# Ln and Exp in place of Newton roots, and a longer hand-written start, in an attention and MLP kernel

## The chip, the cores and the metric

The kernel runs on one core of a Trainium2 chip. The metric is the device time of one execution in microseconds (us), as the median of several executions; the kernel before takes 655.64 us (654.83 to 656.18). The spans quoted from profiles are about 1.8 us shorter than the device times of the same executions.

The engines go by their short names: PE is TensorE, DVE is VectorE, ACT is ScalarE, POOL is GpSimd, SP is SyncE, which here only issues DMAs.

## The reference

There are 8 batches, 12 heads, 448 tokens and a head size of 64. The model width is 768, the hidden width of the MLP 3072.

```python
def rmsnorm(x, g):
    return x / np.sqrt(np.mean(x * x, axis=-1, keepdims=True) + 1e-06) * g
q_n, k_n = rmsnorm(q, g_q), rmsnorm(k, g_k)
attn = softmax(q_n @ k_n.transpose(0, 1, 3, 2) / 8)      # shortened
x = (attn @ v).transpose(0, 2, 1, 3).reshape(8, 448, 768)

mu  = np.mean(x, axis=-1, keepdims=True)
var = np.mean((x - mu) ** 2, axis=-1, keepdims=True)
xn  = (x - mu) / np.sqrt(var + 1e-06) * g_ln
out = x + np.maximum(xn @ w_ch1, 0.0) @ w_ch2
```

Each row needs an inverse square root three times: for q, for k and for the LayerNorm.

## The kernel before

The work is cut into *pairs* of heads (six to a batch, numbered through: pair 6 is the first of batch 1) and *units* of one or two pairs that are loaded and prepared together. Units 0 to 3 are batch 0, units 4 to 6 are batch 1. Preparing a unit means: squares of q and k on ACT, row sums on DVE, the inverse roots, k times the product of the two gains, k split in a high and a low fp16 half, q scaled and copied twice, and the copy of v. Then q and k must be transposed. Units 0 to 4 are transposed by TensorE; from unit 5 on the DMA engines do it.

The program has two phases. In the first, a hand-written list gives the order of all pieces of batch 0's attention. A letter is a piece (b begin, a and c squares, d and e sums, f g h the root, i k times g, j k l m halves and scaled q, v the copy of v, K and Q transposes, S scores, V values, T statistics, L loads, W weights) and a number its unit or pair. Then come 22 matmuls without use, which are meant to keep TensorE's clock up through the first LayerNorm. In the second phase each batch's MLP runs with the next batch's attention spread beside it by a formula.

```python
POOL_HI, POOL_DUP, ACT_Q = (1, 2, 3), (3,), (0,)
ORDER = """
b0 c0 e0 fq0 gq0 a0 hq0 i0 d0 fk0 gk0 j0 b1 c1 a1 i1 l0 m0 k0 hk0 d1 K0 e1 j1 Q0 f1 S0.0 g1 k1
... (cut)
V5.3 V5.4 V5.5 V5.6 T5
""".split()
DMA_UNIT = 5

def _guess(nc, out, a):            # exp of the scaled bit pattern: a first guess of a ** -0.5
    nc.scalar.activation(out, a.bitcast(INT32), AFT.Exp, scale=-0.5 * LN2 * 2.0 ** -23,
                         bias=0.5 * LN2 * (127.0 - 0.043))

def _newton(nc, out, a, t, last=None):
    eng = nc.vector
    for i in range(2):
        eng.tensor_tensor(out=t, in0=out, in1=out, op=ALU.mult)
        eng.scalar_tensor_tensor(out=t, in0=t, scalar=-0.5, in1=a, op0=ALU.mult, op1=ALU.mult)
        eng.scalar_tensor_tensor(out=last if i and last is not None else out, in0=t, scalar=1.5,
                                 in1=out, op0=ALU.add, op1=ALU.mult)
... (cut)
        def kg():
            nc.gpsimd.tensor_tensor(out=c["t"][1], in0=c["t"][1],
                                    in1=sh.gprod.unsqueeze(1).broadcast_to([128, g, D]),
                                    op=ALU.mult)
... (cut)
        def dma_k():
            khl, kU = c["khl"].rearrange("p g e d -> p g (e d)"), self.kU[u % 2]
            ... (cut)
            nc.sync.dma_start_transpose(
                kU[:, 0:1536].rearrange("p (g c) -> p g c", c=128), khl[:, 0:12])
            for e in range(2):
                nc.sync.dma_start_transpose(...)     # the 64 left-over rows; cut
        def dma_q():
            q, qU = c["qn"].rearrange("p g e d -> p g (e d)"), self.qU[u % 2]
            for j in range(3):
                nc.sync.dma_start_transpose(
                    qU.rearrange("p w e s -> p (w e) s")[:, :, ts(j, 128)], q[:, 4 * j:4 * j + 4])
            for e in range(2):
                nc.sync.dma_start_transpose(qU[:, :, e, 384:S], q[64 * e:64 * e + 64, 12:14])
... (cut)
    def run_first(self):
        nc = self.nc
        self.steps, self.mark = self.attention()
        self.pos = 0
        self.first_attention()
        ps = self.ps_m.tile([128, 512], FP32, tag="mlp", name="psW")
        for _ in range(WARM):
            nc.tensor.matmul(ps[:, 0:384], self.sh.id16, ..., start=True, stop=True)
        for op in self.ln_ops(0):
            op()
```

So a unit from 5 on has eight DMA transposes, three for k and five for q, all issued by SyncE, and behind them in the same queue stand the loads of later units. The weights of the MLP are loaded by GpSimd, three pieces of the first matrix (W0 to W2) and two halves of the second (W3, W4). Pair 8 is the first of unit 5, and pair 10 the first of unit 6.

Of the kernel before, what the change touches and what calls it, by code (L numbers as in the profile page):

```python
# [28 lines left out]
POOL_HI, POOL_DUP, ACT_Q = (1, 2, 3), (3,), (0,)  # L29
# [5 lines left out]
b0 c0 e0 fq0 gq0 a0 hq0 i0 d0 fk0 gk0 j0 b1 c1 a1 i1 l0 m0 k0 hk0 d1 K0 e1 j1 Q0 f1 S0.0 g1 k1  # L35
h1 l1 m1 b2 a2 c2 i2 G L4 W0 S0.1 v0 S0.2 d2 K1 S0.3 j2 S0.4 W1 S0.5 W2 e2 f2 g2 Q1 h2 S0.6
V0.0 k2 l2 m2 S1.0 S1.1 b3 S1.2 a3 S1.3 V0.1 V0.2 v2 V0.3 S1.4 K2 V0.4 S1.5 Q2 c3 S1.6 V0.5
V0.6 S2.0 T0 S2.1 d3 V1.0 V1.1 S2.2 V1.2 S2.3 V1.3 e3 V1.4 i3 f3 g3 j3 V1.5 S2.4 h3 S2.5 K3 Q3
V1.6 k3 l3 m3 S2.6 v3 G2 L5 V2.0 S3.0 S3.1 K4 T1 V2.1 W3 S3.2 S3.3 W4 V2.2 V2.3 S3.4 V2.4 Q4
S3.5 V2.5 S3.6 V2.6 K5 S4.0 S4.1 Q5 V3.0 V3.1 S4.2 V3.2 S4.3 V3.3 S4.4 V3.4 S4.5 V3.5 S4.6  # L40
V3.6 S5.0 V4.0 V4.1 T3 S5.1 S5.2 V4.2 S5.3 V4.3 S5.4 V4.4 S5.5 V4.5 S5.6 V4.6 V5.0 V5.1 V5.2
V5.3 V5.4 V5.5 V5.6 T5
""".split()
DMA_UNIT = 5
LN2 = 0.6931471805599453
# [6 lines left out]
def _guess(nc, out, a):  # L52

    nc.scalar.activation(out, a.bitcast(INT32), AFT.Exp, scale=-0.5 * LN2 * 2.0 ** -23,  # L54
                         bias=0.5 * LN2 * (127.0 - 0.043))


def _newton(nc, out, a, t, last=None):

    eng = nc.vector  # L60
    for i in range(2):
        eng.tensor_tensor(out=t, in0=out, in1=out, op=ALU.mult)
        eng.scalar_tensor_tensor(out=t, in0=t, scalar=-0.5, in1=a, op0=ALU.mult, op1=ALU.mult)
        eng.scalar_tensor_tensor(out=last if i and last is not None else out, in0=t, scalar=1.5,
                                 in1=out, op0=ALU.add, op1=ALU.mult)


def _rsqrt(nc, out, a, t, eps, last=None, mul=1.0):

    nc.vector.tensor_scalar(out=a, in0=a, scalar1=mul, scalar2=eps, op0=ALU.mult, op1=ALU.add)  # L70
    _guess(nc, out, a)
    _newton(nc, out, a, t, last)
# [14 lines left out]
class _Fast:  # L87


    def __init__(self, ctx, tc, sh, q, k, v, g_ln, w1, w2, out):  # L90
# [35 lines left out]
        self.late = []  # L126
# [15 lines left out]
    def load_first(self):  # L142
        nc = self.nc
        flat = self.hT.rearrange("p f n -> p (f n)").bitcast(FP32)
        t = [flat[:, 2688 * n:2688 * n + 2688].rearrange("p (w g d) -> p w g d", w=NPAIR, d=D)
             for n in range(2)]
        v = self.p_in.tile([128, 3, 14, D], FP32, tag="qkv", name="vfirst")
        t.append(v.rearrange("p n g d -> p (n g d)").rearrange("p (w g d) -> p w g d", w=NPAIR,
                                                               d=D))
        main = lambda eng, n, p: self.load_main(eng, n, t[n][:, p, 0:6], 0, 2 * p, 2)  # L150
        left = lambda eng, n: self.load_left(eng, n, t[n][:, :, 6], 0, 0, H)
        for n in range(2):
            main(nc.sync, n, 0)
            left(nc.sync, n)
        for n, p in ((1, 1), (0, 1), (1, 2), (1, 3), (0, 2), (0, 3), (2, 0), (2, 1)):
            main(nc.sync, n, p)
        left(nc.sync, 2)
        for n, p in ((1, 4), (1, 5), (0, 4), (0, 5)):
            main(nc.sync, n, p)
        for p in range(2, NPAIR):  # L160
            main(nc.sync, 2, p)
        self.v_first = t[2]
        for u, (b, hs, m) in enumerate(UNITS):
            if b == 0:
                self.loads[u] = [x[:, hs // 2:hs // 2 + m].rearrange("p w g d -> p (w g) d")
                                 for x in t]
# [16 lines left out]
    def prep_ops(self, u):  # L183

# [8 lines left out]
        def begin():  # L193
            c["t"] = self.loads.pop(u)
            c["ssq"] = self.p_n.tile([128, 2, 14], FP32, tag="ssq", name="ssq")[:, :, 0:g]
            c["rr"] = self.p_n.tile([128, 2, 14], FP32, tag="rr", name="rr")[:, :, 0:g]
            c["rt"] = self.p_n.tile([128, 2, 14], FP32, tag="rt", name="rt")[:, :, 0:g]
            o = 7 * UNIT_PAIR[u]
            c["rf"] = self.rr[:, :, o:o + g]
            c["qn"] = self.p_n.tile([128, 14, 2, D], FP16, tag="qn", name="qn")[:, 0:g]  # L200
            c["khl"] = self.p_n.tile([128, 14, 2, D], FP16, tag="khl", name="khl")[:, 0:g]
            self.units[u] = (c["qn"], c["khl"], m)
# [10 lines left out]
        def eps(n=slice(0, 2)):  # L213
            nc.vector.tensor_scalar(out=c["ssq"][:, n], in0=c["ssq"][:, n], scalar1=D * 1e-6,
                                    scalar2=None, op0=ALU.add)

        def guess(n=slice(0, 2)):
            _guess(nc, c["rr"][:, n], c["ssq"][:, n])

        def root(n=slice(0, 2)):  # L220
            _newton(nc, c["rr"][:, n], c["ssq"][:, n], c["rt"][:, n], c["rf"][:, n])

        def kg():
            nc.gpsimd.tensor_tensor(out=c["t"][1], in0=c["t"][1],  # L224
                                    in1=sh.gprod.unsqueeze(1).broadcast_to([128, g, D]),
                                    op=ALU.mult)
# [71 lines left out]
        if UNITS[u][0] == 0:  # L298
            qk = {f"{x}{y}": (lambda f=f, n=n: f(n)) for x, f in zip("fgh", (eps, guess, root))
                  for y, n in (("q", 0), ("k", 1))}  # L300
            return dict(b=begin, a=lambda: square(1), c=lambda: square(0), d=lambda: total(1),
                        e=lambda: total(0), f=eps, g=guess, h=root, i=kg, j=khi, k=klo, l=qn,
                        m=qdup, v=vall if u == 0 else lambda: (vmain(), vleft()), **qk)
        return [lambda: (begin(), square(1), kg()), lambda: total(1), lambda: square(0),
                lambda: total(0), khi, lambda: (eps(), guess(), root(), vmain()), klo,
 qn, qdup, vleft] + (
                    [dma_k, dma_q] if u >= DMA_UNIT else [])
# [104 lines left out]
    def first_attention(self):  # L412
# [3 lines left out]
        nc.scalar.activation(self.sh.warm, self.sh.ones, AFT.Exp)  # L416
        prep = [self.prep_ops(u) for u in range(4)]
        for x in ORDER:
            key, n = x[0], x[1:]
            if key == "L":  # L420
# [10 lines left out]
            elif key in "KQT":  # L431
                dict(K=self.trans_k, Q=self.trans_q, T=self.stats)[key](int(n))
            else:
                prep[int(x[-1])][x[:-1]]()

    def attention(self):

        n, nu, nb0 = B * NPAIR, len(UNITS), NPAIR
        todo, last = {}, -9
        for u in range(5, nu):  # L440
            p, m = UNIT_PAIR[u], UNITS[u][2]
            st = max(7 * (p - 2 - m) + 2, last + 1, 7 * nb0)
            e = max(7 * (p - 2) - 1, st + 5)
            last = e
            ops = self.prep_ops(u)
            k = len(ops) - 2
            for x, op in enumerate(ops):
                todo.setdefault(st + (e - st) * x // (k - 1) if x < k else e + 1 + x - k, []).append(op)
            if u < nu - 2:
                todo.setdefault(e, []).append(lambda u=u: self.load_unit(u + 2))  # L450
        steps, mark = [], [0]

        steps += [[op] for op in self.prep_ops(UNIT_PAIR.index(nb0)) if op is not None]
        steps[-1].append(lambda: self.load_unit(6))
        steps += [[lambda: self.trans_k(nb0)], [lambda: self.trans_q(nb0)]]
        for p in range(nb0, n + 1):
            for i in range(7):
                c = []
                if i == 0 and p < n and p % NPAIR == 0:
                    c.append(lambda b=p // NPAIR: self.batch(b))  # L460
                c += todo.pop(7 * p + i, [])
                if p < n:
                    c.append(lambda p=p, i=i: self.scores(p, i))
                if p > nb0:
                    for x in {0: (), 1: (0, 1)}.get(i, (i,)):
                        c.append(lambda p=p, x=x: self.values(p - 1, x))
                if p > nb0 + 1 and i == 1 and (p - 1) % NPAIR:
                    c.append(lambda p=p: self.stats(p - 2))
                if p + 1 < UNIT_PAIR[DMA_UNIT]:
                    if i == 2:  # L470
                        c.append(lambda p=p: self.trans_k(p + 1))
                    if i == 4:
# [3 lines left out]
                steps.append(c)  # L476
# [35 lines left out]
    def ln_ops(self, b):  # L512
# [19 lines left out]
        def root():  # L532
            _rsqrt(nc, st[:, 0:n, 0], mv[:, 0:n, 1], st[:, 0:n, 1], 1e-6 * XS * XS,
                   self.rs[:, b, 0:n], XS * XS)

        def first():
            aggregate()
            for t in range(3):
                norm(t)
            if b:  # L540
                root()

        def trans(t):
            self.ln_trans(b, c["xn", t], t)
            if t + 3 < n:
                norm(t + 3)

        return [first] + [lambda t=t: trans(t) for t in range(n)] + ([] if b else [root])
# [78 lines left out]
    def run_first(self):  # L627
# [5 lines left out]
        ps = self.ps_m.tile([128, 512], FP32, tag="mlp", name="psW")  # L633
        for _ in range(WARM):
            nc.tensor.matmul(ps[:, 0:384], self.sh.id16,
                             self.v16.rearrange("p s h j d -> p (s h j d)")[:, 0:384],
                             start=True, stop=True)
        for op in self.ln_ops(0):
            op()

    def run_rest(self):
        steps, mark, upto = self.steps, self.mark, self.upto
        tail = 10
        for b in range(B):
# [10 lines left out]
            for i, (cost, emit) in enumerate(chunks):  # L655
# [5 lines left out]
                if self.pos >= goal and items is None:  # L661
                    items = self.ln_ops(b + 1)
# [224 lines left out]
```

## Time and profile before

| | kernel before |
|---|---|
| device time | 655.64 us |
| span of the profile | 654.0 us |
| first MLP starts (first matmul into psH) | 64.6 us |
| second MLP starts | 156.0 us |
| two batches in the steady part | 143.9 us |
| DVE and ACT busy in the whole span | 341.3 and 355.7 us |

The page's rows of tenths, the stages, the waits and the issuing queue are shown in the prediction. (The clock there is what the throttle granted, 1 for full speed; the DMA share adds up the times of packets, which overlap, so it can be above 1.) In the page's rows, DMA is the mean busy share of the 16 DMA engines, in tenths for 40 slices of 16.35 us.

```profile
DMA  8999955653543534662454444554252220010011
```

The row reads 8 or 9 for five slices, until about 80 us, while unit loads and weights arrive together. Unit 5's transposes in this kernel are issued at 91.3 us, after that.

### The profile page before, as it was taken

Reading aid. Unit: us, or ns where it says so; the run is one execution under the profiler, and the core shown is the slowest. Engines: PE = TensorE matmul, PEld = TensorE weight load, DVE = VectorE, ACT = ScalarE, POOL = GpSimd, SP = SyncE. Lnnn points to the kernel's source line nnn. Section 1 sums busy time; section 2 is a strip of 40 time slices with the busy share of each in tenths; the row PEclk is TensorE's granted clock in tenths of the full one; section 3 lists DMA queues with packets and bytes.
Section 4 is the critical chain, followed back from the end, with each engine's and each line's share of the span. In section 5 each row is a group of like instructions: output and inputs, shape, how many; then the busy total and the mean of one; then the engine's idle time right before and its main releaser. Section 6 shows DMA issues by size and latency. Waiting matters only on the chain.

```text
span 654.0 us, 11757 instructions
## 1 busy us (share of the span) xinstructions
PE 595.6 (91%) x4528; PEld 351.7 (54%) x4528; DVE 341.3 (52%) x873; ACT 355.7 (54%) x639; POOL 103.0 (16%) x114
## 2 busy tenths in 40 slices
PE   1678766989999999999999999999999999999995
PEld 1355433555556666665556666655556666654563
DVE  6987762766246655664436736673535722380011
ACT  3655765752775449744874368635874277314300
POOL 2630522220202202220211202220221100000000
PEclk9979997999999999999999999999999999999999
DMA  8999955653543534662454444554252220010011
GB/s 232 241 200 203 229 133 140 134 138 105 142 112 91 129 99 110 124 163 92 102 130 120 106 116 110 112 138 139 52 141 69 73 65 6 26 49 1 1 49 52
DMA packets 149838, 73.13 MB, mean 112 GB/s; under 512 B 99728, under 2 KB 144784, under 8 KB 149776
## 3 DMA queue, kind: packets, MB, share of 16 engines
q1 hardware_dynamic: 140960, 62.82, 38.1%
q0 software_dynamic: 8528, 9.44, 8.6%
q8 instruction: 37, 0.61, 0.4%
q14 instruction: 25, 0.20, 0.1%
q10 hardware_dynamic: 288, 0.07, 0.0%
HBM read 52.36 MB, written 11.01 MB: 97 GB/s over the span
## 4 chain that ended last, share of the span: by engine, by line
PE 69%; DVE 13%; SPq 5%; issue 5%; DMA 3%; ACT 2%; POOL 1%; DVEq 0%; ACTq 0%; POOLq 0%
PE psH L574 29%; PE psC L587 24%; PE psS L351 6%; PE oA L380 4%; DVE xn L529 3%; SPq L264 2%; DVE khl L235 2%; DVE stat L509 2%; PE oB L382 1%; SPq L140 1%; DMA hT<-in_q_dram 1%; PE psX L556 1%; PE psS L354 1%; SPq L132 1%; PE psS L355 1%
## 5 line engine op out<-in xcount | busy, mean ns | idle before, releaser
L357 ACT ACTIVATE E<-psS,rr_all 128x448 f16<-128x448 f32 x336 | 207.9, 634 | 80.5 <-PE psS L351 71.7
L574 PE MATMUL psH<-xnT,w 128*128 128x512 f16 (+1 forms) x1152 | 246.1, 354 | 0.7 <-DVE stat L70 0.7
L587 PE MATMUL psC<-w,hT 128*128 128x384 f16 x1344 | 241.4, 326 | 1.9 <-DVE x L591 1.9
L576 ACT ACTIVATE hT<-psH 128x384 f16<-128x384 f32 (+1 forms) x192 | 104.9, 547 | 115.7 <-PE psH L574 114.1
L587 PEld LDWEIGHTS <-hT 128*128 128x128 f16 x1344 | 124.1, 98 | 73.1 <-issue 2.4
L574 PEld LDWEIGHTS <-w 128*128 128x128 f16 x1152 | 104.9, 98 | 84.8 <-issue 3.1
L351 PE MATMUL psS<-qU,kU 128*128 128x448 f16 x288 | 103.4, 366 | 24.2 <-DMA qU<-qn 11.5
L380 PEld LDWEIGHTS <-E 128*128 128x128 f16 x1008 | 72.5, 100 | 54.9 <-issue 9.0
L224 POOL TENSOR_TENSOR qkv<-qkv,gprod 128x896 f32<-128x896 f32 x21 | 43.7, 2082 | 344.9 <-issue 240.7
L591 DVE SCALAR_TENSOR_TENSOR x<-psC,rs_all,x 128x384 f32<-128x384 f32 x48 | 29.6, 617 | 81.5 <-PE psC L587 80.7
L380 PE MATMUL oA<-v,E 128*128 128x65 f16 x864 | 67.9, 196 | 1.3 <-DVE x L397 1.0
L211 DVE TENSOR_REDUCE ssq<-khl 128x14 f32<-128x896 f32 (+1 forms) x25 | 26.2, 1047 | 70.7 <-ACT khl L208 70.7
L382 PE MATMUL oB<-v,E 128*128 128x65 f16 x288 | 52.6, 196 | 0.1
L395 DVE RECIPROCAL rec_all<-oA 128x6 f32<-128x6 f32 x48 | 9.4, 195 | 78.5 <-PE oA L380 78.3
L351 PEld LDWEIGHTS <-kU 128*128 128x128 f16 x288 | 28.2, 100 | 38.9 <-issue 15.5
L211 DVE TENSOR_REDUCE ssq<-qn 128x14 f32<-128x896 f32 (+1 forms) x25 | 26.1, 1046 | 20.1 <-ACT qn L208 20.0
L382 PEld LDWEIGHTS <-E 128*128 128x128 f16 x336 | 33.0, 98 | 0.4 <-DVE xl L402 0.2
L78 DVE SCALAR_TENSOR_TENSOR qn<-qkv,rr_all 128x256 f16<-128x256 f32 (+2 forms) x81 | 27.3, 395 | 1.6
L397 DVE TENSOR_TENSOR x<-oA,rec_all 128x384 f32<-128x384 f32 x48 | 26.8, 558 | 1.7 <-DVE rec_all L396 0.2
L509 DVE BATCH_NORM_STATS2 stat<-x 128x6 f32<-128x256 f32 x72 | 26.5, 416 | 0.7
L54 ACT ACTIVATE stat<-stat 128x3 f32<-128x3 int32 (+1 forms) x8 | 1.7, 210 | 45.4 <-DVE stat L70 45.4
L235 DVE TENSOR_TENSOR khl<-qkv,khl 128x896 f16<-128x896 f32 x21 | 22.8, 1087 | 4.3 <-ACT khl L232 4.3
(95 smaller groups left out, 427.4 us busy)
## 6 DMA issues: line engine op xcount, KB each, us to landing
qkv<-in_k_dram SPq DMA_DIRECT2D x21, 384.0 KB, 3.3
qkv<-in_q_dram SPq DMA_DIRECT2D x21, 384.0 KB, 3.9
qkv<-in_v_dram SPq DMA_DIRECT2D x21, 384.0 KB, 4.4
out_dram<-x SPq DMA_DIRECT2D x20, 384.0 KB, 2.5
w<-in_moe_w_ch_dram POOLq DMA_DIRECT2D x3, 1536.0 KB, 17.9
w<-in_moe_w_ch_dram POOLq DMA_DIRECT2D x2, 2304.0 KB, 27.0
qU<-qn SPq DMA_TRANSPOSE x100, 2.4
out_dram<-x SPq DMA_DIRECT2D x8, 192.0 KB, 2.2
```

Of the source, the lines that this page charges most:

```text
L211: nc.vector.tensor_reduce(out=c["ssq"][:, n], in_=c["sq", n], axis=AX.X, op=ALU.add)
L224: nc.gpsimd.tensor_tensor(out=c["t"][1], in0=c["t"][1], in1=sh.gprod.unsqueeze(1).broadcast_to([128, g, D]), op=ALU.mult)
L235: nc.vector.tensor_tensor(out=c["khl"][:, :, 1], in0=c["t"][1], in1=c["khl"][:, :, 0], op=ALU.subtract)
L351: nc.tensor.matmul(ps[:, 0:S], c["main"][:, ts(i, 128)], q[:, ts(h, S)], start=True, stop=True)
L357: nc.scalar.activation(out=c["E"][:, i], in_=ps[:, 0:S], func=AFT.Exp, scale=self.rr[:, 1, g:g + 1], bias=EXP_BIAS)
L380: nc.tensor.matmul(oA[:, t, cs], E[:, i, ts(t, 128)], rhs, start=(i == 0 and t == 0), stop=(i == 6 and t == 2))
L382: nc.tensor.matmul(oB[:, cs], E[:, i, 320:448], rhs, start=(i == 0), stop=(i == 6))
L509: nc.vector.bn_stats(out=self.st[b][:, t, 6 * s:6 * s + 6], in_=x[:, 256 * s:256 * s + 256])
L574: nc.tensor.matmul(ps[:, 0:N], sh.w1[:, dc, ts(f, 128)], xnT[:, dc, 0:N], start=(dc == 0), stop=(dc == NDC - 1))
L576: nc.scalar.activation(out=hT[:, f, 0:N], in_=ps[:, 0:N], func=AFT.Relu)
L587: nc.tensor.matmul(ps[:, 0:384], hT[:, f, ts(t, 128)], sh.w2[:, f, ts(g, 384)], start=(f == 0), stop=(f == NFF - 1))
L591: nc.vector.scalar_tensor_tensor(out=x[:, ts(g, 384)], in0=ps[:, 0:384], scalar=self.rs[:, b, t:t + 1], in1=x[:, ts(g, 384)], op0=ALU.mult ...
```

## The change

It has three parts. **Part 1** replaces six Newton operations, the addition of eps and the first guess by two activations: a root is exp(-0.5 ln(x)). Both functions are in one table set, which is loaded once at the start. **Part 2** writes a new list. It is packed differently, it goes on into batch 1, and it runs pair 6 and the preparation of units 4 and 5 while the first LayerNorm (A, N, X, R) is under way, in place of the 22 warming matmuls. **Part 3** puts k times g of units 0 and 1 on VectorE. (The change also parks batch 0's v in the memory of the second weight matrix; this is among what the diff below leaves out.) The intent is to take load off VectorE, to fill the gap before the first MLP, and to have batch 1 under way when that MLP begins.

```diff
-POOL_HI, POOL_DUP, ACT_Q = (1, 2, 3), (3,), (0,)
+DVE_KG, POOL_HI, POOL_DUP, ACT_Q = (0, 1), (1, 2, 3, 4), (1, 2, 4, 5), (0, 1)
 ORDER = """
... (the old list goes; of the new one the parts that the argument needs)
+S0.1 k1 S0.2 S0.3 L4 W0 L5 K1 c2 e2 S0.4 W1 V0.0 i2 S0.5 Q1 g2 l2 V0.1 j2 S0.6 S1.0 m2 S1.1
+j3 S3.2 W3 W4 S3.3 k3 V2.2 l3 m3 S3.4 K4 b4 Q4 V2.3 a4 V2.4 S3.5 V2.5 V2.6 S3.6 Q5 V3.0 S4.0
+T3 V5.2 V5.3 S5.6 V5.4 V5.5 Q6 V5.6 S6.0 S6.1 S6.2 S6.3 T5 V6.0 z5 A N0 V6.1 V6.2 d5 N1 S6.4
+c5 V6.3 V6.4 i5 j5 X0 S6.5 X1 N2 e5 X2 k5 S6.6 V6.5 g5 l5 m5 x5 V6.6 R y5
 """.split()
... (cut)
-def _rsqrt(nc, out, a, t, eps, last=None, mul=1.0):
-    nc.vector.tensor_scalar(out=a, in0=a, scalar1=mul, scalar2=eps, op0=ALU.mult, op1=ALU.add)
-    _guess(nc, out, a)
-    _newton(nc, out, a, t, last)
+def _rsqrt(nc, out, a, t, eps, mul=1.0):
+    nc.scalar.activation(t, a, AFT.Ln, scale=mul, bias=eps)
+    nc.scalar.activation(out, t, AFT.Exp, scale=-0.5)
... (cut)
-            nc.gpsimd.tensor_tensor(out=c["t"][1], in0=c["t"][1],
+            (nc.vector if u in DVE_KG else nc.gpsimd).tensor_tensor(
... (cut)
-        for _ in range(WARM):
-            nc.tensor.matmul(...)
-        for op in self.ln_ops(0):
-            op()
```

In the new list x5 and y5 are unit 5's DMA transposes of k and of q, z5 is the copy of its v, and i5 and j5 are its k times g and its high half.

## The prediction

> **What bounds the kernel now.** I first read the page's busy shares, then its slices.
>
> ```profile
> PE 595.6 (91%) x4528; PEld 351.7 (54%) x4528; DVE 341.3 (52%) x873; ACT 355.7 (54%) x639; POOL 103.0 (16%) x114
> ...
> PE   1678766989999999999999999999999999999995
> ...
> DVE  6987762766246655664436736673535722380011
> ```
>
> TensorE (PE) is full from about slice 11 on (16.35 us a slice) and not before. So the time is TensorE's work after about 156 us plus a start that something else sets. I then asked for busy time by stage: first attention (batch 0), first LayerNorm gap, first MLP with batch 1's attention beside it, and one later period of two batches.
>
> ```profile
> 6.00:57.20 51.20, 32.67 (x300) 20.84 (x301) 41.83 (x91) 31.55 (x57) 20.31 (x22) 0.93 1.05 231
> 57.20:64.56 7.36, 5.31 (x44) 3.15 (x42) 6.50 (x17) 1.63 (x3) 0.00 (x0) 1.00 1.26 214
> 64.56:156.00 91.44, 70.95 (x565) 42.98 (x566) 58.17 (x146) 53.54 (x98) 23.54 (x26) 0.94 0.67 146
> ...
> 156.00:299.90 143.90, 142.12 (x1100) 84.36 (x1099) 79.95 (x208) 87.97 (x158) 23.18 (x24) 1.00 0.49 123
> ```
>
> The columns are stretch and length, then busy us (and instructions) of PE, weight loads, DVE (VectorE), ACT (ScalarE) and POOL (GpSimd), granted clock, DMA share, GB/s. In the later periods PE is busy 142.1 of 143.9 us: nothing done to DVE or ACT there can gain much. In the first attention DVE is busy 41.8 of 51.2 us; the gap adds 7.4 us in which 5.3 us of PE is mostly 22 warming matmuls without use; the first MLP takes 91.4 us with PE busy only 71.0. The waits of PE from 65 to 156 us name the missing 20.5 us:
>
> ```profile
> PE psS L351 <- DMA qU<-qn: 11.5, 3, 8.8
> PE psS L351 <- ACT E L357: 4.4, 7, 1.1
> ...
> PE tr L329 <- DVE qn L275: 1.8, 1, 1.8
> ```
>
> The first is the wait for transposes by DMA. Its reason is in the timeline of the DMA-issuing queue of SyncE:
>
> ```profile
> 102.41 0.45 SPq L132 DMA_DIRECT2D qkv<-in_k_dram  x1
> ...
> 108.19 1.83 SPq L254 DMA_TRANSPOSE kU<-khl  x1
> 110.07 2.50 SPq L257 DMA_TRANSPOSE kU<-khl  x2
> 112.67 4.90 SPq L264 DMA_TRANSPOSE qU<-qn  x3
> 117.62 2.51 SPq L267 DMA_TRANSPOSE qU<-qn  x2
> 120.30 0.46 SPq L132 DMA_DIRECT2D qkv<-in_k_dram  x1
> ```
>
> A unit (two pairs of heads) needs nine loads, 5.8 us, and eight transposes, 12.1 us with their gaps: 17.9 us of this queue, with no pause between units (the next ones begin at 120.30 and 137.83). In the steady part two batches have six units in 143.9 us, 24 us for each, so the queue is no bound there; in the first MLP it is, because the first unit's transposes begin late (91.34) and all later ones stand behind them.
>
> **What the Trainium skill says.** "ScalarE: Activation LUTs", section "Table sets: the hidden batching unit", lists a set with both exp and ln, so that the pair needs no switch. The one table load in the trace took 1.28 us, as the section on its cost says; the changed program also has just one. "SBUF — State Buffer", section "Who interferes with whom": a VectorE instruction with two SBUF inputs contends with a GpSimd instruction that reads SBUF, and the later one blocks wholly. The trace agrees: a Newton step of usually 0.17 us stood 1.94 us until a GpSimd product ended.
>
> ```profile
> 17.25 2.08 POOL L224 TENSOR_TENSOR hT<-hT,gprod 128x896 f32<-128x896 f32 x1 [2.17 <-ACT khl L208]
> ...
> 17.41 1.94 DVE L64 SCALAR_TENSOR_TENSOR rr_all<-rt,rr 128x14 f32<-128x14 f32 x1
> ```
>
> "TensorE: Matmul & The Clock Gate", section "What's actually happening": after an idle window the array gets half its clock. The trace agrees: after the 9 us wait before 102 us, six 384-column matmuls take 2.12 us in place of 1.14. "DMA: Bandwidth & Descriptors", section "DMA Transpose (X-bar)": plain transposes go through SyncE or ScalarE only; in this trace all stand on SyncE, so that queue's 17.9 us cannot be shed, only started earlier.
>
> **Part 1, Ln and Exp.** It removes one eps addition and six Newton operations per root from DVE: groups of 10.6, 10.2, 8.9, 6.6 and 5.7 us for the units, 8.9 us for LayerNorm, about 51 us over the span. It adds one small activation per root: 33 of about 0.23 us, 7.6 us on ACT. After 156 us nearly all of this lies beside PE work; PE waits there only 4.2 us in all, none of it named for a root. I give that 0 to 1 us. Before 64.56 us the chains as timed, with their stalls, are 2.1, 2.2, 3.0, 2.4, 1.3 (units) and 1.1 us (LayerNorm): 12.0 of DVE's 48.3 us.
>
> **Part 2, the longer first list.** The first stage now also prepares units 4 and 5 and runs pair 6. DVE: 48.3 - 12.0 = 36.3; unit 4: two sums, low half and scaled q at 1.09, 4.4; unit 5: 4.6; pair 6: evacuation 1.2, k and q copies 1.3; k times g of units 0 and 1, two of 0.6 (part 3), 1.2; less one q copy and some duplicates moved to ACT and GpSimd, 0.9. Sum 48.1 us. ACT: 31.6 + 1.6 = 33.2; four squares of 0.95, 3.8; seven exponentials of 0.63, 4.4; a high half and a q copy, 1.9; Ln/Exp, 2.3. Sum 45.6. So the warming matmuls and the gap are filled, at no more DVE work. At the share of before (48.3 of 58.6 us, 82%) the first MLP would begin at 6 + 48.1/0.82 = 64.6. But ACT has risen from 57% to near the same load, and the two feed each other. I choose 67 (79% and 75%).
>
> In the first MLP: scores of pairs 7 to 12 (six of 3584 columns), values of 7 to 11 (five of 2080), MLP 110592 columns, transposes about 4900: 147,400 columns, or 61.4 us at the 2.4 GHz that the skill's clock page gives. The steady period has 331,500 columns, 138.1 us, in 143.9: 1.04. So 64 us of PE. Against it:
> - ACT in the half with the first weight matrix: about 30 steps, 23 with an exponential. Each has 0.63 + 0.79 x 0.5 (Relu) + 3.4/14 (preparation) = 1.27 us, against PE's 1.11. About 4 us more.
> - SyncE's queue: unit 5's transposes are issued before the MLP and no longer hold it up. Units 6 and 7 follow at 17.9 us, bounded also by buffers that come free only as their units are prepared. Unit 7's land about 50 us into the MLP and are wanted at about 47.5: some 2 us, as before (2.27).
>
> Sum 64 + 4 + 2 = 70; LayerNorm's small waits at the end are partly inside the 1.04, and before took 18.3 us from that last wait to the next MLP, which gives 50 + 18 = 68. I take 69.
>
> **Part 3, k times g on VectorE for units 0 and 1.** 0.61 us instead of 1.13 on GpSimd, earlier in the first chain (two of the stalls above began there). With the two shorter roots, the first score matmul moves from 15.0 to about 13.4 us; this is inside the 67.
>
> **Sum.** The second MLP begins at 67 + 69 = 136 instead of 156: 20 us off, and up to 1 us later. 655.6 - 20.5 = 635.
>
> **Rivals.** (a) The work only moves: DVE, ACT and PE at half clock all fill the first stage, and the MLP begins at 75 or later. For it: three engines at high load, DMA share over 1 from 20 to 80 us (units 4 and 5 load beside 9 MB of weights). Against: 12 us of Newton leave. Time 643 to 646. (b) SyncE's queue stays the bound in the first MLP: unit 6's loads wait for buffers, and the 17.9 us chain starts late as before. For it: five loads and transpose groups must pass by the second batch's first scores. Against: unit 5 is ahead by its whole group. D would be 76: time 642. (c) The list is better packed than before, the first MLP begins at 62 and takes 66: time 627. (d) ScalarE becomes the bound later through the added activations: 7.6 us against 143.9 - 88 us of its idle time per period; I give it under 1 us.
>
> **Range and chances.** The start is uncertain by about 4 us, the MLP by about 5, together 6 to 7; eight in ten within 626 to 645. Two per cent faster is 642.5, which needs 13 of the 20.5 us: 0.87. Within 2%: 0.11. Slower would take a failing accuracy check and the fallback, or a first stage past 100 us: 0.02.
>
> **What would show it.** Right: one table load; no Newton groups; PE's wait for DMA-transposed q falls from 11.5 us to under 4; no warming matmuls; the first MLP matmul at 64 to 70 us; the second MLP at 131 to 141; later periods of 143 to 144 us. Wrong: the first MLP matmul after 75 us with DVE idle, a wait for weights or loaded k in the first stage, or periods that change by over 1 us.

## The result

| | before | predicted | after |
|---|---|---|---|
| device time, us | 655.6 | 635 (626 to 645) | 648.8 (647.8 to 649.4) |
| first MLP starts | 64.6 | 67 | 66.4 |
| first MLP lasts | 91.4 | 69 | 83.5 |
| second MLP starts | 156.0 | 136 | 149.9 |
| two later batches | 143.9 | 143.9 | 143.9 |

The result is correct, and 1.0% faster: the ratio is 0.9895, with a 95% interval of 0.9878 to 0.9912. (A ratio is the mean time of one kernel's runs over that of the other's in the same rounds, so it is not quite the ratio of the medians quoted.) That is within 2%, and the predicted range does not hold it. The kernel is 13.8 us slower than predicted, and the table says where: the first MLP took 14.5 us more than its 69.

The page of the changed kernel, first its busy times with their share of the span and the number of instructions, then its rows of tenths:

```profile
PE 594.3 (92%) x4506; PEld 349.6 (54%) x4506; DVE 293.0 (45%) x633; ACT 362.7 (56%) x673; POOL 103.1 (16%) x116
...
PE   2873957999999999999999999999999999999995
...
DVE  5795504573425625672434625582443621380011
...
DMA  8999985554255354564255355455243230010011
```

VectorE lost 48 us of work, and TensorE is still not full before about slice 8. The sixth slice of the DMA row (81 to 97 us) reads 8 where before it read 5. The stages of the changed kernel, in the columns that the prediction explains (stretch and length, busy us and instructions of PE, weight loads, DVE, ACT and POOL, granted clock, DMA share, GB/s):

```profile
6.00:66.43 60.43, 35.89 (x368) 22.22 (x369) 44.34 (x81) 43.15 (x82) 27.36 (x31) 0.88 1.14 239
66.43:149.90 83.47, 71.35 (x516) 42.54 (x515) 40.81 (x86) 45.92 (x88) 16.63 (x19) 0.90 0.74 155
149.90:293.80 143.90, 142.44 (x1102) 84.47 (x1100) 70.33 (x153) 89.63 (x166) 23.20 (x24) 1.00 0.50 118
```

In the first MLP 516 matmuls remain, against 565 before, so pair 6 did leave it. But PE is busy 71.4 us with them, at a granted clock of 0.90, and idle for 12.1. Its longest wait from 66.43 to 150 us (total us, times, longest):

```profile
PE psS L326 <- DMA qU<-qn: 10.5, 2, 6.5
```

This is the wait that was to fall from 11.5 to about 2. It stands at 10.5. This is the issuing queue of SyncE (start, length, line, kind, what is moved):

```profile
26.29 7.45 SPq L125 DMA_DIRECT2D qkv<-in_k_dram  x2
...
64.74 9.19 SPq L235 DMA_TRANSPOSE kU<-khl  x1
73.97 2.50 SPq L238 DMA_TRANSPOSE kU<-khl  x2
...
77.20 7.84 SPq L245 DMA_TRANSPOSE qU<-qn  x3
85.09 2.52 SPq L248 DMA_TRANSPOSE qU<-qn  x2
```

Unit 5's eight transposes are issued early, at 64.74 us, as planned: 26.6 us earlier than before. But they then stand in the queue until 87.6 and have landed at 88.7 us, 24 us after the first was issued, where the same eight took 12.0 in the kernel before. Meanwhile the last half of the second weight matrix is on its way; it lands at 85.3 us. TensorE's timeline shows what it costs (start, length, engine, line, work, and in brackets the idle time before and its releaser):

```profile
87.99 0.53 PE L326 MATMUL psS<-qU,kU 128*128 128x448 f16 x1 [6.55 <-DMA qU<-qn]
88.32 2.12 PE L564 MATMUL psH<-xnT,w 128*128 128x384 f16 x6
```

The first scores of pair 8 wait 6.55 us, and after the wait six MLP matmuls take 2.12 us, where six of the same size took 1.14 just before it (80.30 us). Unit 6's transposes follow in the same queue at 99.9 us, after the loads that stood behind unit 5's. TensorE waits again at 111 us (3.9 us), and again runs at half speed afterwards. The stretches in which the granted clock was 0.50 (the columns as above):

```profile
66.43:69.47 3.04, 3.04 (x17) 1.86 (x16) 2.49 (x9) 0.83 (x4) 1.07 (x2) 0.50 1.26 213
...
87.99:93.36 5.37, 5.37 (x24) 2.62 (x25) 0.00 (x0) 1.79 (x4) 0.00 (x0) 0.50 0.44 105
...
111.26:117.26 6.00, 6.00 (x29) 3.08 (x30) 0.00 (x0) 2.43 (x5) 0.00 (x0) 0.50 0.56 151
```

In the first of them the first MLP begins; the clock had been at 0.50 since 59.2 us. The kernel before, with its 22 warming matmuls, was granted 1.00 at that point.

The start, too, was not set by what the prediction had in mind. The chain of what released what, between 40 us and the first MLP (start, length, what):

```profile
...
48.59 11.38 DMA qkv<-in_v_dram
...
60.47 2.08 POOL qkv L205
62.57 0.95 ACT khl L213
63.52 0.69 ACT xnT L549
```

Unit 5's v is issued at 48.59, behind other loads in SyncE's queue, and lands at 60 us. GpSimd copies it, and only then, in its own order, multiplies k by g (60.47). ACT's high half of k waits for that, and behind it in ACT's order stands the copy that the first MLP reads. So the start came at 66.4 us, as predicted, through a load and not through busy VectorE and ACT.

### The profile page after: what moved, and what is told of

It reads as the page before. It is cut to its first block, busy times and chain, and to the rows that moved or that the text cites. A ratio compares the mean times of both kernels' runs of the same rounds, so it can differ in the third digit from the quotient of the medians.

```text
span 647.3 us, 11504 instructions
## 1 busy us (share of the span) xinstructions
PE 594.3 (92%) x4506; PEld 349.6 (54%) x4506; DVE 293.0 (45%) x633; ACT 362.7 (56%) x673; POOL 103.1 (16%) x116
## 4 chain that ended last, share of the span: by engine, by line
PE 74%; DVE 8%; SPq 7%; DMA 4%; ACT 3%; issue 2%; POOL 0%; ACTq 0%; DVEq 0%; POOLq 0%
PE psH L564 32%; PE psC L577 25%; PE psS L326 7%; PE oA L355 4%; SPq L125 4%; DVE xn L519 3%; DMA qkv<-in_v_dram 2%; PE oB L357 1%; SPq L245 1%; SPq L117 1%; DVE stat L499 1%; PE psX L546 1%; DVE khl L216 1%; ACT E L332 1%; PE psS L329 1%
## 5 line engine op out<-in xcount | busy, mean ns | idle before, releaser
L564 PE MATMUL psH<-xnT,w 128*128 128x512 f16 (+1 forms) x1152 | 250.4, 358 | 0.0
L332 ACT ACTIVATE E<-psS,rr_all 128x448 f16<-128x448 f32 x336 | 207.8, 632 | 71.1 <-PE psS L326 64.6
L326 PE MATMUL psS<-qU,kU 128*128 128x448 f16 x288 | 104.3, 365 | 17.7 <-DMA qU<-qn 10.5
L581 DVE SCALAR_TENSOR_TENSOR x<-psC,rs_all,x 128x384 f32<-128x384 f32 x48 | 29.5, 617 | 85.7 <-PE psC L577 85.1
L370 DVE RECIPROCAL rec_all<-oA 128x6 f32<-128x6 f32 x48 | 9.3, 194 | 98.3 <-PE oA L355 98.1
L262 POOL CAST v<-qkv 128x768 f16<-128x768 f32 x21 | 17.4, 828 | 35.6 <-PE oB L357 19.6
```

What stands on the lines that cost most here:

```text
L326: nc.tensor.matmul(ps[:, 0:S], c["main"][:, ts(i, 128)], q[:, ts(h, S)], start=True, stop=True)
L332: nc.scalar.activation(out=c["E"][:, i], in_=ps[:, 0:S], func=AFT.Exp, scale=self.rr[:, 1, g:g + 1], bias=EXP_BIAS)
L564: nc.tensor.matmul(ps[:, 0:N], sh.w1[:, dc, ts(f, 128)], xnT[:, dc, 0:N], start=(dc == 0), stop=(dc == NDC - 1))
L581: nc.vector.scalar_tensor_tensor(out=x[:, ts(g, 384)], in0=ps[:, 0:384], scalar=self.rs[:, b, t:t + 1], in1=x[:, ts(g, 384)], op0=ALU.mult ...
```

## The experiments

My theory after the result: *the transposes were moved to where the weight loads fill the DMA engines; the first MLP is held by their landing, and whatever only moves the start is lost there.* The rivals: the start itself is the cost (the chain through v or the order of the weights); one of the parts costs more than it brings; SyncE's queue is the bound whatever else is in flight. The kernels ran in four groups, each on one chip with its own runs of the kernel before (medians 656.4 to 657.6 us). Times are medians.

The last part of the second weight matrix to land, the landing of unit 5's transposes and the two later milestones are from the profiled executions, in us:

| run | time | first MLP | last weights land | unit 5 transposes | pair 10 scores | second MLP |
|---|---|---|---|---|---|---|
| before | 655.6 | 64.6 | 80.3 | 91.3 to 103.3 | 120.1 | 156.0 |
| changed | 648.8 | 66.4 | 85.3 | 64.7 to 88.7 | 111.3 | 149.9 |
| e1_w2_late | 648.3 | 62.7 | 94.5 | 62.6 to 95.6 | 114.3 | 150.3 |
| e2_v_copy_after_kg | 648.9 | 63.1 | 85.7 | 65.7 to 89.2 | 111.7 | 150.3 |
| e3_ln_exp_only | 650.2 | 53.8 | 85.4 | 85.7 to 98.0 | 115.0 | 151.0 |
| e4_order_only | 650.8 | 69.8 | 86.4 | 70.5 to 90.5 | 112.0 | 149.6 |
| e6_quarter_of_w2 | 636.1 | 66.7 | 59.2 | 64.9 to 77.2 | 99.4 | 136.4 |
| e5_pe_unit5 | 638.5 | 67.7 | 86.7 | none by DMA | 102.0 | 138.8 |

### e1_w2_late: the second weight matrix later

```diff
-S3.2 W3 W4 S3.3
+S3.2 S3.3
-i5 j5 X0
+i5 W3 W4 j5 X0
```

> The changed kernel with the two loads of the second weight matrix issued about 28 us later, after unit 5's k times g. Theory A (the DMA engines are full until about 79 us, and these two loads, 15 us earlier than before and 9.4 MB of reads, hold up unit 5's loads and its transposes): unit 5's v lands by 48 us instead of 59, the first MLP matmul moves from 66.4 to 57 to 61 us, the first DMA-transposed q wait falls from 6.5 us to under 2, and the time falls by 8 to 14 us to 635 to 641. Rival B (GpSimd's and ScalarE's order is what costs: k times g of unit 5 stands behind the copy of v): v still lands late because the loads of unit 6 and of the first weight matrix fill the queue, the first MLP matmul stays at 64 or later, time within 3 us of 648.8. Rival C (SyncE's own issue order): time the same within 3 us.

The time is 648.27 us, ratio 0.9878 (0.9852 to 0.9905), the same as the change. The first MLP does begin earlier, at 62.7 us, and unit 5's loads land at 53.0 instead of 60.0. But the weights now travel exactly when the transposes do, and one group of three stands 9.5 us in the queue:

```profile
76.95 9.54 SPq L245 DMA_TRANSPOSE qU<-qn  x3
```

They take 33 us from first issue to landing, end 1.1 us after the last weights, and cost one wait of 18.0 us. What the start gained was lost again.

### e2_v_copy_after_kg: the copy of v out of the way of k times g

```diff
-V6.0 z5 A N0
+V6.0 A N0
-X1 N2 e5
+X1 N2 z5 e5
```

> The changed kernel with unit 5's copy of v on GpSimd moved behind its k times g and the high half. Theory A: k lands at about 50 us whatever the order, so the first MLP matmul moves at most from 66.4 to 60-61 us, but unit 5's transposes still issue into full DMA engines and still take about 20 us; the wait for transposed q stays over 4 us and the time falls by 2 to 5 us. Rival B: k times g starts at 51 instead of 60.5, the first MLP matmul and all after it move by 6 to 9 us and the time falls by as much.

648.95 us, ratio 0.9881 (0.9851 to 0.9912). The start moves 3.3 us forward to 63.1, so the chain shown above was real. The second MLP starts at 150.3 all the same, since unit 5's transposes land at 89.2. The rival that the start is the cost falls here, together with e1.

### e3_ln_exp_only: part 1 alone, on the kernel before

```diff
 def _rsqrt(...):
-    nc.vector.tensor_scalar(out=a, in0=a, scalar1=mul, scalar2=eps, ...)
-    _guess(nc, out, a)
-    _newton(nc, out, a, t, last)
+    nc.scalar.activation(t, a, AFT.Ln, scale=mul, bias=eps)
+    nc.scalar.activation(out if last is None else last, t, AFT.Exp, scale=-0.5)
```

(The pieces f and h of the old list become empty and g the whole root; the table set is loaded as in the change.)

> The kernel before with the inverse roots by Ln and Exp and nothing else; order list, units and k times g as before. My prediction's part 1 says: 12 us of DVE work leave the first stage; if DVE bounded it, the first MLP matmul moves from 64.6 to 58 to 61 us, and the time by 3 to 6 us to 650 to 653; after that the wait for transposed q (11.5 us) stays. If DMA or ScalarE bounds the stage, the first MLP matmul stays within 2 us and the time within 2 us of 655.6. Later periods 143 to 144 us either way.

650.18 us, ratio 0.9906 (0.9864 to 0.9948). The two stages, and what TensorE waited for between 65 and 152 us:

```profile
6.00:53.80 47.80, 33.38 (x341) 20.88 (x342) 36.71 (x72) 34.39 (x66) 20.27 (x22) 1.00 1.10 244
53.80:151.00 97.20, 72.57 (x564) 43.64 (x565) 50.62 (x97) 54.53 (x103) 23.63 (x26) 0.91 0.75 155
```

```profile
PE psS L333 <- DMA qU<-qn: 15.0, 3, 11.7
```

The shorter roots alone start the first MLP 10.8 us earlier, much more than I had expected. Then the MLP takes 97.2 us instead of 91.4 and gives half of it back: 15.0 us go to the wait for the transposes. They are issued at 85.7 us, as the weights have just landed (85.4), and take 12.3 us. So eight transposes take about 12 us when no weights are in flight, late or early.

### e4_order_only: parts 2 and 3 with the Newton roots

```diff
 def _rsqrt(nc, out, a, t, eps, mul=1.0):
-    nc.scalar.activation(t, a, AFT.Ln, scale=mul, bias=eps)
-    nc.scalar.activation(out, t, AFT.Exp, scale=-0.5)
+    nc.vector.tensor_scalar(out=a, in0=a, scalar1=mul, scalar2=eps, op0=ALU.mult, op1=ALU.add)
+    _guess(nc, out, a)
+    _newton(nc, out, a, t)
```

> The changed kernel with Newton's roots on VectorE in place of Ln and Exp; order list, units and k times g on VectorE as in the change. Theory A: DVE stood idle for want of data between 48 and 66 us, so that Newton's 12 us and its stalls partly fit there: the first MLP matmul at 68 to 72 us, time 650 to 655. If DVE bounds: the first MLP matmul at 76 to 80, time 658 to 662.

650.77 us, ratio 0.9922 (0.9898 to 0.9946). The start is 69.8 us, the latest of all, and the second MLP begins at 149.6, within the others. From e3 to e4 the start differs by 16 us and the second MLP by 1.4. Part 1 alone gains 0.9%, parts 2 and 3 alone 0.8%, and all together 1.05 to 1.2% (over three groups of runs): they do not add up. The wait for unit 5's transposes is one reason; e11 below shows another.

### e5_pe_unit5: TensorE transposes unit 5 in the changed kernel

```diff
-DMA_UNIT = 5
+DMA_UNIT = 6
-g5 l5 m5 x5 V6.6 R y5
+g5 l5 m5 V6.6 R
-self.kU[u % 2]      (and qU; three places)
+self.kU[(u - DMA_UNIT + 1) % 2]
```

> The changed kernel with unit 5 transposed on TensorE as units 0 to 4 are, so that no transposes of unit 5 stand on SyncE's queue (units 6 and 7 swap their target buffers so that unit 6 need not wait for pairs 8 and 9). Theory D (the first MLP is gated by when unit 5's DMA transposes land, which is when the weights have landed, at 85 to 95 us in all five orders tried, whatever the first MLP's start): pair 8's first scores move from 88 to 78 to 81 us, pair 10's from 111 to 95 to 102, the second MLP from 150 to 137 to 142, time 636 to 642, although TensorE does 1.5 us more. Rival E (ScalarE or the first MLP's own work bounds it): time within 3 us of 648.8. Rival F (the gate only passes to unit 6's transposes): pair 8 early, pair 10 at 108 or later, time 645 to 648.

638.46 us, ratio 0.9715 (0.9691 to 0.974): some 10 us better than the change, with no weight load moved. The first MLP holds 30 more matmuls (the transposes) and lasts 71.1 us:

```profile
67.70:138.80 71.10, 68.34 (x546) 42.47 (x544) 43.05 (x87) 46.09 (x88) 16.07 (x19) 0.96 0.73 156
```

The granted clock rose from 0.90 to 0.96. The wait for DMA-transposed q is 0.8 us. Unit 6's transposes, the first by DMA, are issued at 90.7 us and take 12.5.

### e6_quarter_of_w2: fewer weight bytes (wrong on purpose)

```diff
-            out=self.sh.w2[:, :, ts(g, 384)],
-            in_=self.w2[:, ts(g, 384)].rearrange(...))
+            out=self.sh.w2[:, 0:6, ts(g, 384)],
+            in_=self.w2[0:768, ts(g, 384)].rearrange(...))
-                ... sh.w2[:, f, ts(g, 384)],
+                ... sh.w2[:, f % 6, ts(g, 384)],
```

> The changed kernel with only a quarter of the second weight matrix loaded, used four times over: the result is WRONG ON PURPOSE, the work is the same, 7 MB less is read. Theory D: the DMA engines are free by about 60 us, unit 5's k and v land some 5 to 10 us sooner (first MLP matmul at 58 to 62), its transposes take about 12 us in place of 24 and land by 74 to 78, pair 8 does not wait, the second MLP begins at 135 to 142 and the time is 634 to 642. Rival: if SyncE's queue alone sets the transposes, they still land at 85 or later and the time stays within 3 us of 648.8.

Its output is wrong (relative error 1.39); its instructions are the same in number and shape, and only the last two weight loads move a quarter of their bytes. One round gave 636.13 us, ratio 0.968 (0.9653 to 0.9707). The queue and the first MLP:

```profile
64.91 1.53 SPq L235 DMA_TRANSPOSE kU<-khl  x1
66.49 2.51 SPq L238 DMA_TRANSPOSE kU<-khl  x2
...
69.72 3.81 SPq L245 DMA_TRANSPOSE qU<-qn  x3
73.58 2.51 SPq L248 DMA_TRANSPOSE qU<-qn  x2
```

```profile
66.70:136.40 69.70, 65.34 (x516) 40.12 (x515) 40.72 (x86) 45.69 (x87) 15.95 (x19) 0.98 0.58 131
```

The same eight transposes, issued at the same moment (64.9 against 64.7 us), take 12.3 us instead of 24. The first MLP takes 69.7 us: the 69 of the prediction, with the same 516 matmuls. This is the experiment that shows the cause, and the rival that SyncE's queue is the bound whatever else is in flight falls with it. It also splits the cost: in the changed kernel PE was busy 71.35 - 65.34 = 6.0 us longer (clock 0.90 against 0.98) and waited 10.5 - 2.3 = 8.2 us longer for the transposes (2.3 is the same wait in this run). Together these are 14.2 us; the stages differ by 13.8. What e6 shows is that the load of the second matrix is the cause. That it is the time of the 16 DMA engines that runs out is argued from their share (1.09 from 66.43 to 92 us in the changed kernel, 0.68 here), not isolated.

One expectation missed: the start did not move (66.7 us). Unit 5's loads still land at 59.6. What holds them was not tested; in e1, with the second matrix issued later, they landed at 53.0.

### e7_w4_late: only the last half of the second matrix later

```diff
-S3.2 W3 W4 S3.3
+S3.2 W3 S3.3
+            if u == 6:
+                todo.setdefault(46, []).append(lambda: self.load_w2(1))
```

> The changed kernel with only the second half of the second weight matrix issued later, on GpSimd after unit 6's k times g (about 70 us in place of 32); it is needed only at about 122 us. Theory D: what lands last before the transposes is then the first half, at about 68 us; unit 5's transposes land at 76 to 82 in place of 88.7, unless the late half, issued at 70, meets the last five of them. Second MLP at 140 to 147, time 639 to 646. If instead its issue meets them as in the run with both halves late: time 647 to 650.

646.81 us, ratio 0.9849 (0.9818 to 0.988). W4 is issued at 73.2 us and lands at 95.6, in time for its use. But the transposes, with the first half still in flight and then this one, land at 86.4, only 2.3 us earlier, and later than I had expected. Moving weights about in a full window is worth 0.3 to 0.5% here, and the intervals overlap.

### e8_kg_gpsimd and e14_kg_gpsimd_again: part 3 undone

```diff
-DVE_KG, POOL_HI, POOL_DUP, ACT_Q = (0, 1), ...
+DVE_KG, POOL_HI, POOL_DUP, ACT_Q = (), ...
```

> The changed kernel with k times g of units 0 and 1 back on GpSimd, Ln and Exp and the order list kept. My part 3 says about 0.5 us of the first chain for each: the first score matmul at 14.2 to 15.5 in place of 13.6. Theory D: nothing of this passes the gate at 88 us, the time stays within 1 us of 648.8. Rival (the first stage bounds): 2 to 3 us slower.

645.77 us, ratio 0.9823 (0.9803 to 0.9844): better than the change, where I had expected no more than 1 us either way. The first score matmul came at 13.4 us, not at 14.2 to 15.5, so the half microsecond that part 3 was to save in the first chain is not there.

> The changed kernel with k times g of units 0 and 1 on GpSimd, beside the changed kernel in the same rounds. If the part costs: ratio 0.980 to 0.984 against 0.987 to 0.990, and pair 10's scores at 109 to 110 us against 111. If not: the two ratios within 0.002.

645.94 us, ratio 0.9836 (0.9813 to 0.9858), against 649.05 and 0.9878 (0.9857 to 0.9898) for the changed kernel (e15): 3.1 us. The two intervals just touch, but e8 and e14 agree with each other, and three groups of the changed kernel gave 0.9895, 0.9881 and 0.9878. Part 3 costs about 0.4%. What the trace shows beside it, first e15 and then e14, on GpSimd:

```profile
16.01 1.83 POOL L473 DMA_DIRECT2D w<-in_moe_w_ch_dram  x2
```

```profile
15.16 1.13 POOL L205 TENSOR_TENSOR hT<-hT,gprod 128x448 f32<-128x448 f32 x1
...
17.36 1.82 POOL L473 DMA_DIRECT2D w<-in_moe_w_ch_dram  x2
```

With the product gone from GpSimd, it issues the first weight loads 1.35 us earlier. Unit 4's loads then land at 43.3 us instead of 36.3, and unit 5's at 60.9 instead of 57.6. A later issue of the weights would let the loads of the units pass first. That is an argument from the order of events; I did not isolate it. Unit 5's transposes land almost as before (88.0 in e14, 88.9 in e15). The gain comes through unit 6's, as e14's expectation said: in a queue that is 2 us ahead they are issued at 98.1 instead of 100.2 us and land at 110.3 instead of 112.6, pair 10's scores begin at 109.1 instead of 111.4, and the second MLP at 146.7 instead of 149.9.

### e9_changed_again and e15_changed_third: the changed kernel unaltered

> The changed kernel itself, unaltered, as the yardstick of this round on the same chip: ratio to before 0.985 to 0.992; first MLP matmul at 62 to 67 us, pair 8 at 88 us, second MLP at about 150. If its ratio is near 0.982, the gain of the run with k times g on GpSimd was the chip and not the edit.

649.02 us, ratio 0.9881 (0.986 to 0.9903).

> The changed kernel unaltered, as the yardstick of these rounds: ratio 0.987 to 0.990, second MLP at 149 to 150 us.

649.05 us, as told above. The changed kernel gave medians within 0.3 us of each other in three groups of runs.

### e10_combined: e5, e2 and e8 together

```diff
-DMA_UNIT = 5
+DMA_UNIT = 6          (with the rest of e5)
-V6.0 z5 A N0
+V6.0 A N0             (with the rest of e2)
-DVE_KG, ... = (0, 1), ...
+DVE_KG, ... = (), ...
```

> Unit 5 transposed on TensorE, with unit 5's copy of v behind its k times g, and k times g of units 0 and 1 on GpSimd. Theory D: with the gate gone the first MLP's start passes through: first MLP matmul at 62 to 64 in place of 67.7, second MLP at 134 to 137 in place of 138.8, time 634 to 637, ratio 0.966 to 0.970. Rival: a gate at unit 6's transposes (103 us in that run) now holds; then time 638 and ratio 0.971 as with unit 5 on TensorE alone.

638.34 us, ratio 0.9714 (0.9693 to 0.9734), no better than e5 alone. The first MLP begins at 58.8 us, 9 earlier than in e5, and the second at 137.5, only 1.3 earlier. TensorE waits 6.3 us for unit 6's transposes, which land at 101.3 (103.2 in e5). The gate has moved on by one unit.

### e11_lnexp_pe5: part 1 alone, old list, unit 5 on TensorE

```diff
-DMA_UNIT = 5
+DMA_UNIT = 6
-            k = len(ops) - 2
+            k = len(ops) - 2 if u >= DMA_UNIT else len(ops)
```

(on e3, with the same change of buffer index as in e5)

> The kernel before with Ln and Exp and unit 5 on TensorE, with the old order list and units. First MLP matmul at 54 us as with Ln and Exp alone; pair 8 no longer waits (96.5 there). If the order list were needed for the gain: time 645 or more. If the gate was the whole obstacle: pair 8 at 82 to 86, second MLP at 138 to 144, time 636 to 643.

637.94 us, ratio 0.9711 (0.9691 to 0.9731). With unit 5 off the DMA engines, the old list and the new one end equal: 637.9 against 638.3 and 638.5. Unit 6's transposes land at 103.5 us here. The first MLP starts at 54.8 us and lasts 83.2, where e5's starts at 67.7 and lasts 71.1: 138.0 and 138.8. There the new list only moves work from behind the start to before it.

### e12_before_pe5: the same on the kernel before

```diff
-DMA_UNIT = 5
+DMA_UNIT = 6          (with the rest of e11, but with the Newton roots)
```

> The kernel before with only unit 5 transposed on TensorE; Newton, old list. The gate is in the kernel before as well (pair 8 at 102 us, waits of 11.5 us): without it pair 8 at 92 to 94, the second MLP at 145 to 149, time 645 to 649, that is about what the whole change brought. If pair 10's transposes take over as the gate: 651 or more.

645.77 us, ratio 0.9825 (0.9799 to 0.9852). A change of a few lines gains 11 to 12 us in the kernel before, where the whole three-part change gained 7 to 8.5. The gate was there already; the change did not create it. From e12 to e11 the Ln and Exp roots add 7.8 us, against 6.3 in e3, with the gate. The new list with Newton roots and unit 5 on TensorE was not run.

### e13_pe_units5_6: e10 with unit 6 on TensorE as well

```diff
-DMA_UNIT = 6
+DMA_UNIT = 7
+            pieces = pieces[:k] if u < DMA_UNIT else pieces
```

> The combined kernel with unit 6 transposed on TensorE too. If unit 6's transposes are the next gate (pair 10 waited 6.3 us for them at 100 us): pair 10 at 94 to 97, second MLP at 131 to 135, time 632 to 636, ratio 0.962 to 0.968. If ScalarE or TensorE itself bounds the first MLP by now: second MLP at 137 or later, ratio 0.970 or more.

642.43 us, ratio 0.9778 (0.9755 to 0.9801): worse than e10, a miss. Pair 10 starts earlier than anywhere (94.5 us), but then ACT stands:

```profile
109.12 0.95 ACT L196 ACTIVATE qn<-qkv 128x896 f32<-128x896 f32 x1 [9.11 <-DMA qU<-qn]
```

This square for a later unit writes a buffer that unit 7's transposes are still reading. ACT takes its work in order, so the exponentials behind it wait too, and TensorE waits 8.4 us for them. The gate shows itself again, from its other side: the DMA transposes do not only deliver late, they also hold their source buffer.

### e16_lnexp_pe5_6: e11 with unit 6 on TensorE as well

```diff
-DMA_UNIT = 6
+DMA_UNIT = 7
```

> The kernel before with Ln and Exp, old list, units 5 and 6 on TensorE. If unit 6's transposes are the next gate also here (2.8 us of waits): pair 10 at 100 to 101, second MLP at 134 to 137, ratio 0.966 to 0.970; the new order list, with pair 6 done before the first MLP, should then be ahead by 2 to 4 us for the first time. If the lists still tie, it is worth nothing even without the gates.

632.88 us, ratio 0.9637 (0.9617 to 0.9657), correct: the fastest of all, 3.6% better than the kernel before and 2.4% better than the changed one. I had not expected the old list to win. Its stages:

```profile
6.00:53.40 47.40, 33.13 (x340) 20.77 (x340) 36.63 (x71) 34.23 (x66) 20.29 (x22) 1.00 1.10 243
53.40:133.80 80.40, 72.76 (x620) 46.34 (x621) 55.03 (x99) 54.97 (x103) 24.49 (x26) 0.98 0.81 170
```

The first MLP starts at 53.4 us and none of TensorE's waits from there to 134 us is for a DMA; the largest in total is for exponentials, 5.4 us in six waits. The transposes cost TensorE nothing in the sum: it is busy 592.7 us in the whole span, less than the 594.3 of the changed kernel, with a clock of 0.98 instead of 0.90 in the first MLP. Whether the new list could do better without e13's buffer wait was not tried.

## Why the prediction was wrong

**The step that failed** is the second of the two added to TensorE's 64 us: "SyncE's queue: unit 5's transposes are issued before the MLP and no longer hold it up." They were issued before the MLP (64.7 against 66.4 us) and did hold it up. The prediction took the queue time of eight transposes, 12.1 us, from a stretch at 108 to 120 us, when the weights had long landed, and used it at 65 us, when they had not. Measured: 24.0 us in the changed kernel, 20.0 in e4, 23.5 in e2 and 33.0 in e1, each with weight loads in flight, and 12.0, 12.3 and 12.3 in the kernel before, e3 and e6 with none. The term "some 2 us" was 10.5 us of waits, and with them went the term of "64 us of PE": 71.4, since 5.4 us of work after the first wait and 6.0 after the second ran at half clock. E6 puts both back, 65.3 us of PE and a stage of 69.7.

That e6 comes so near to 69 is in part luck. The 4 us added for ACT are not there: in e6 TensorE waits 0.9 us for exponentials. PE's 64 are 65.3, with half clock until 68.9 us, which the sum had left out. A further step was wrong: the queue's 17.9 us "cannot be shed, only started earlier". TensorE took the transposes of one unit in e5 and of two in e16.

The mechanism could have been read in advance. The Trainium skill, "DMA: Bandwidth & Descriptors", section "Issuing engines are not separate DMA queues", says that DMAs started by different engines run on the same 16 DMA engines and interleave. I had quoted the page for who may issue a transpose, and rival (a) names the DMA share above 1 up to 80 us; I used it only against the loads, not against the transposes that the new list puts in that stretch. With weights in flight, the share from 66.4 to 92 us was above 1.

```profile
66.43:92.00 25.57, 18.84 (x109) 10.74 (x108) 8.60 (x18) 13.44 (x28) 5.47 (x7) 0.83 1.09 179
```

The queue itself adds to it. In the trace SyncE's issues wait on eight semaphores in turn, so that each waits for the landing of the issue eight before it: those at 53.54, 58.48 and 63.96 us began 0.01 to 0.02 us after that landing. But this does not explain the long issues. The one at 26.29 us stood 5.85 us (7.45 is with the next), although the issue eight before it had landed at 21.29, and the first transpose stood 9.19 us (1.53 in e6) after its waits had ended. What holds an issue so long is not shown; it happens while the weights are in flight. Whatever it is, what stands behind in the queue is late, too: unit 6's transposes are issued at 99.9 us here and at 88.2 in e6.

**A common gate** explains most of the parts. In all runs of the table the second MLP follows the first scores of pair 10 by 36 to 39 us, while the start of the first MLP moved over 16 us. Where pair 8 waits, that is in all but e5 and e6, what sets pair 10 is the end of unit 5's and then unit 6's transposes. So the sum of the prediction, start plus a fixed length, was wrong in form: the length was not fixed, and what the start gained, the wait took. The gate is not all: without it (e5, e11) the new list still gained nothing over the old one.

**Right**, by its own marks: the start was predicted at 67 and came at 66.4. But that came through unit 5's v load at 60 us and not through "79% and 75%" of busy VectorE and ACT (they were 44.3 and 43.2 of 60.4 us, 73% and 71%). The number was right and its reason was not; the prediction had named a wait for weights or loaded k in the first stage as a sign of a wrong step; it was loaded v. The later periods were 143.9, as said, and from 149.9 us on the span has 497.4 us against 498.0 after 156.0 before: 0.6 us of the "0 to 1". Part 1's sizes nearly hold: in e3, which has part 1 alone, VectorE lost 46.3 us (predicted 51) and ACT gained 6.6 (7.6). The groups of the root in the changed kernel are these, with one table load:

```profile
L56 ACT ACTIVATE rt<-ssq 128x28 f32<-128x28 f32 (+2 forms) x26 | 5.9, 228 | 0.0
...
L57 ACT ACTIVATE rr_all<-rt 128x28 f32<-128x28 f32 (+2 forms) x26 | 5.8, 225 | 0.8
...
L391 ACT ACT_TABLE_LOAD x1 | 1.3, 1283 | 1.7 <-PEq L854 1.7
```

Each root is two activations of 0.23 us, as estimated. The first scores came at 13.6 us (predicted 13.4), but not through part 3: without it they came at 13.4 in e8 and e14, and these two runs show part 3 to cost 3 us later.

**The rivals.** (b), the queue stays the bound, with 76 us for the first MLP and 642 in all, was nearest in kind, but it looked for the cause in loads that wait for buffers, and was 7 us short. (a) named the full DMA engines but expected the start to slip; it did not. (c), a better packed list, is refuted for the whole. (d), ACT as a later bound, is refuted by the unchanged periods. **The chances** (0.87 for more than 2%) treated start and length as independent errors of 4 and 5 us. A single missed collision moved the length by 14.5, so they were too narrow.

## What to carry to other kernels

A transfer's duration belongs to the stretch in which it was timed: before you move it earlier, read the DMA share of the stretch that it moves into, and what else will be in flight there. When two parts of a change each gain alone and little together, look for a gate that both run into, and remove the gate first; here handing two units from the DMA engines to TensorE was worth more than the rest, and it showed which half of the change had a gain of its own. In an issuing queue that works in order, one slow transfer delays everything behind it.

## What the Trainium skill lacked or had wrong

- "DMA: Bandwidth & Descriptors": its section "DMA Transpose (X-bar)" gives no time for small transposes within SBUF beside other traffic. Here the eight of a unit took 20 to 33 us from first issue to last landing with weight loads in flight, and 11.4 to 14.8 us in all groups of all runs once the weights had landed. Its section "Issuing engines are not separate DMA queues" calls the time to initiate a DMA usually small beside the DMA itself. Here the issue of unit 5's first transpose took 9.19 of the 18.9 us from its start to the landing, and 1.53 of 3.4 us in e6.
- "ScalarE: Activation LUTs", section "What ACT_TABLE_LOAD costs": for an activation with immediate scale and bias it has 186 ns + 0.833 ns for each element, 209 ns for 28 elements. With numbers for scale and bias in the kernel, the 23 roots of 28 elements took 232 ns for Ln and 227 for Exp.
